# Zero matmuls in planned TensorE gaps, a new division of phi, and new due times, in a two-layer linear-attention and gated-MLP kernel

## The chip, the cores and the metric

The kernel runs on one core of one Trainium2 chip. The metric is device time in microseconds (us), median over runs. Every comparison is between runs of the same job on the same chip, unless it says otherwise.

Engines: PE is TensorE, ACT is ScalarE, DVE is VectorE, POOL is GpSimd, SP is SyncE, which here only issues DMAs. "Clock" is the TensorE clock that the chip granted, as a share of full speed.

## The reference

Two layers, each a linear attention A and a gated MLP B with residuals, on x of 2048 tokens by 512. Cut to what matters:

```python
qkv = x @ wqkv                                   # 32 heads of 16
pq, pk = q @ w_phi, k @ w_phi                    # per head
phi = concat([softmax(p), softmax(-p)])          # of pq and of pk
kv, z = phi_k^T v, sum over tokens of phi_k      # the "sum over tokens"
o = (phi_q kv) / (phi_q z + 1e-6);  A = o @ wo
B = (relu(x @ W_gate) * (x @ W_up)) @ W_down
x = x + A(layernorm(x)); x = x + B(layernorm(x))  # twice
```

The sum over tokens (named `kvz`) accumulates over all 16 tiles of 128 tokens before any query can be answered. Everything until then is the head of the kernel.

## The kernel before

The kernel records operations, each with a cost estimate and a due time. At build time a planner walks them in simulated time and picks, engine by engine, what goes next; the due times come from a search by annealing over that planner. On the chip only the resulting order counts, engine by engine.

```python
POOL_HEAD = 30.2
PHI = dict(POOL=[("POOL", 16)] * 4, DVE=[("DVE", 64)], BOTH=[("DVE", 32), ("POOL", 16), ("POOL", 16)])
PHI0 = ["POOL"] * 15 + ["BOTH"]     # who computes phi, for the 16 tiles of layer one
DUE = ( ... )                       # one due time per operation
# ...
    c_z = op("DVE", dve(512, 4), -9, lambda: nc.vector.memset(p_h.tiles[0][:, 0:512], 0.0), name="zero", port=True)
# ...
    wps = Buf(p_q)
    op("PE", mm(8, 512), 0, lambda: [nc.tensor.matmul(
        wps.t[:], lhsT=p_h.tiles[0][:, 0:P], rhs=p_h.tiles[0][:, 0:512],
        start=True, stop=True) for _ in range(8)], [c_z], [wps], name="warm")
# ... for each tile of 128 tokens: key product, exp on ACT (ek), sum (sk), 1/sum, then phi:
            for e, n in PHI[phi_eng]:
                q, cost = (nc.vector, dve(n * DH)) if e == "DVE" else (nc.gpsimd, (POOL_HEAD * n, POOL_HEAD * n + 10))
                parts.append(op(e, cost, due, lambda q=q, lo=lo, n=n: phi(q, lo, n), [a], [] if lo else [ph],
                                [ek, sk] + ([ph] if lo else []), name="phi", port=True))
                lo += n
# ... at the end:
    order = arrange(ops)
    with tc.manual_schedule():
        for o in order:
            o.emit()
```

The eight `warm` matmuls of zeros keep PE active while the first data are loaded (1.19 to 4.79 us in the trace, 0.43 us apart). In layer one GpSimd does phi in four instructions of 16 heads per tile, and in the last tile VectorE takes half. (The code counts 64 heads to a tile: each of the 32 heads of the reference stands there twice, once for each of its two softmaxes.)

The softmax here doesn't subtract the row's maximum and nothing guards it: scores larger than these inputs give would overflow.

## Time and profile before

| | before |
|---|---|
| three runs | 396.55 us median (396.2 to 397.12) |
| the profiled run | 398.66 us, span 396.9 us, mean clock 0.991 |
| matmuls of 512 columns, start to start | 0.43 us at clock 0.50, 0.216 us at 1.00 |

The page of the kernel before: the span, the busy line of PE (busy us, share, instructions), and from the 40 slices the PE line and the clock line, where 9 is 90% or more.

```profile
span 396.9 us, 7609 instructions
...
PE 381.3 (96%) x2780; PEld 232.0 (58%) x2827; DVE 269.9 (68%) x663; ACT 257.1 (65%) x683; POOL 40.7 (10%) x72
...
PE   8799899999999999999999999999899999999996
...
PEclk9699999999999999999999999999999999999999
...
PE 81%; ACT 8%; DMA 5%; DVE 4%; issue 1%; DVEq 0%; ACTq 0%
```

PE is busy nearly always and makes up 81% of the chain of waits (the last line). The second slice of the clock line has a 6: there the clock was not full. A caution for the PE count: this trace has 2780 matmul records and 2827 weight loads, so 47 matmul records are missing, and small gaps without a named wait are not to be believed.

The table of stretches for the dip (stretch, length, busy us of PE, PEld, DVE, ACT and POOL with the instruction count of each, then the clock, the DMA share and GB/s; PEld is the loading of weights into TensorE):

```profile
8.64:12.05 3.41, 1.62 (x12) 0.55 (x9) 3.41 (x11) 2.54 (x9) 0.00 (x0) 1.00 0.57 108
12.05:15.47 3.42, 2.23 (x13) 1.42 (x13) 3.28 (x6) 2.06 (x9) 1.32 (x3) 0.50 0.19 41
15.47:18.88 3.41, 3.41 (x11) 1.18 (x9) 2.64 (x5) 1.55 (x3) 1.03 (x2) 0.50 0.73 212
```

In the first stretch PE was busy for 1.62 of 3.41 us. In the following two it ran at half clock. The stretches follow the clock record of this trace, which changes at 5.21, 12.04 and 18.86 us. A stretch of 3.41 us is called a window here. The timeline of PE (start, length, line, what, and in brackets the idle time before it with what ended it) shows the gaps and the slow matmuls:

```profile
8.29 0.59 PE L663 MATMUL b<-Wk,xnTA 128*128 128x512 bf16 x2
9.17 0.38 PE L663 MATMUL b<-Wk,xnTA 128*128 128x512 bf16 x1 [0.28 <-ACT Wk L587]
9.73 0.38 PE L663 MATMUL b<-Wk,xnTA 128*128 128x512 bf16 x1 [0.18 <-DVE Wk L587]
11.43 0.72 PE L623 MATMUL b<-ident,xn 128*128 128x128 bf16 x8 [1.33 <-DVE xn L643]
13.34 1.49 PE L663 MATMUL b<-Wk,xnTA 128*128 128x512 bf16 x3 [1.19 <-ACT rsA L640]
...
17.18 1.86 PE L663 MATMUL b<-Wk,xnTA 128*128 128x512 bf16 x4
```

The group of four key products at 17.18 took 1.86 us; elsewhere such a group takes 1.03 us. The waits of PE over the whole run (what waited, for what, us in total, times, longest):

```profile
PE b L783 <- DMA oT<-o: 2.2, 3, 1.0
PE b L736 <- DMA xnTA<-xn: 1.5, 1, 1.5
PE b L623 <- DVE xn L643: 1.3, 1, 1.3
PE b L663 <- ACT rsA L640: 1.2, 1, 1.2
PE q L580 <- DVE hT L560: 1.2, 1, 1.2
PE b L783 <- ACT oT L587: 1.0, 2, 0.6
...
```

All lines of this list together make 9.5 us.

### The profile page before, as it was taken

The page shows a single profiled execution, that of the slowest core. Times are in us where ns is not written, and L with a number is a line of the kernel's source. Part 1 is how long each engine was busy: PE and PEld are TensorE (multiplying, and loading weights), DVE is VectorE, ACT ScalarE, POOL GpSimd, SP SyncE. Part 2 cuts the span into 40 slices and gives each one's busy share as a digit, 9 for nine tenths or more (in the row PEclk, how much of TensorE's full clock was granted, in tenths as well). Part 3 has the DMA queues.
Part 4 walks back from the last instruction along what each step waited for, and adds up shares of the span by engine and source line. Part 5 has one row for each costly group of instructions (what it writes and reads, how often), then busy time and mean ns, then how long its engine had stood idle before and what let it go on. Part 6 is the DMA issues. An engine that isn't in the chain of part 4 may idle for free.

```text
span 396.9 us, 7609 instructions
## 1 busy us (share of the span) xinstructions
PE 381.3 (96%) x2780; PEld 232.0 (58%) x2827; DVE 269.9 (68%) x663; ACT 257.1 (65%) x683; POOL 40.7 (10%) x72
## 2 busy tenths in 40 slices
PE   8799899999999999999999999999899999999996
PEld 4354555876655454646666655577675444547585
DVE  6898645889958797953575887778799881322232
ACT  5699999975656557654646769997565545164141
POOL 0286891000000000000000002000000000000000
PEclk9699999999999999999999999999999999999999
DMA  8339760122423311210102000013333512101110
GB/s 238 104 90 192 197 195 0 25 52 49 93 28 67 42 40 40 41 20 15 29 20 55 0 15 0 2 28 61 67 61 80 99 24 28 59 0 28 40 49 28
DMA packets 60870, 22.84 MB, mean 58 GB/s; under 512 B 52672, under 2 KB 59808, under 8 KB 60832
## 3 DMA queue, kind: packets, MB, share of 16 engines
q1 hardware_dynamic: 60416, 21.95, 25.2%
q8 instruction: 22, 0.36, 0.4%
q10 hardware_dynamic: 416, 0.39, 0.3%
q14 instruction: 16, 0.13, 0.1%
HBM read 7.91 MB, written 2.10 MB: 25 GB/s over the span
## 4 chain that ended last, share of the span: by engine, by line
PE 81%; ACT 8%; DMA 5%; DVE 4%; issue 1%; DVEq 0%; ACTq 0%
PE b L847 32%; PE b L881 18%; PE b L663 6%; PE b L669 6%; PE b L783 5%; PE b L736 4%; PE q L699 3%; DMA oT<-o 3%; PE b L823 3%; PE q L754 2%; ACT Eq L740 2%; ACT N L761 2%; DMA xnTA<-xn 1%; ACT DS L761 1%; ACT ek L666 1%
## 5 line engine op out<-in xcount | busy, mean ns | idle before, releaser
L847 PE MATMUL b<-xnTB,wgu 128*128 128x128 bf16 (+2 forms) x1194 | 151.6, 279 | 0.4
L847 PEld LDWEIGHTS <-wgu 128*128 128x128 bf16 x1200 | 98.0, 98 | 45.9 <-issue 0.3
L881 PE MATMUL b<-wd,hT 128*128 128x512 bf16 (+2 forms) x344 | 83.4, 372 | 1.0
L851 ACT ACTIVATE gu<-b 128x512 bf16<-128x512 f32 x83 | 49.9, 605 | 39.3 <-PE b L847 39.2
L854 ACT CAST gu<-b 128x512 bf16<-128x512 f32 (+1 forms) x83 | 48.8, 590 | 36.3 <-PE b L847 35.8
L857 DVE TENSOR_TENSOR hT<-gu 128x512 bf16<-128x512 bf16 (+1 forms) x83 | 34.0, 411 | 43.0 <-ACT gu L854 42.7
L683 POOL TENSOR_TENSOR phiK<-ek,sk 128x256 bf16<-128x256 bf16 x66 | 40.0, 639 | 203.8 <-ACT sk L679 198.3
L881 PEld LDWEIGHTS <-hT 128*128 128x128 bf16 (+1 forms) x363 | 34.3, 98 | 31.2 <-DVE hT L857 0.4
L674 DVE TENSOR_REDUCE sk<-ek 128x64 f32<-128x1024 bf16 x32 | 38.7, 1213 | 19.9 <-ACT ek L666 19.7
L761 ACT CAST N<-q 128x384 bf16<-128x384 f32 (+1 forms) x96 | 44.4, 531 | 4.9 <-PE q L754 3.8
L888 DVE SCALAR_TENSOR_TENSOR X<-b,rsB,X 128x512 bf16<-128x512 f32 (+1 forms) x33 | 23.5, 726 | 26.2 <-PE b L881 26.1
L666 ACT ACTIVATE ek<-b 128x512 bf16<-128x512 f32 x64 | 36.0, 604 | 8.2 <-PE b L663 8.0
L740 ACT ACTIVATE Eq<-b 128x512 bf16<-128x512 f32 x64 | 37.8, 657 | 1.6 <-PE b L736 1.2
L663 PE MATMUL b<-Wk,xnTA 128*128 128x512 bf16 x124 | 33.7, 393 | 1.8 <-ACT rsA L640 1.2
L783 PE MATMUL b<-wo,oT 128*128 128x512 bf16 x119 | 31.6, 379 | 3.6 <-DMA oT<-o 2.2
L669 PE MATMUL b<-wv,xnTA 128*128 128x512 bf16 x125 | 32.8, 387 | 0.2
L736 PE MATMUL b<-xnTA,Wq 128*128 128x512 bf16 x122 | 30.6, 379 | 1.8 <-DMA xnTA<-xn 1.5
L754 PE MATMUL q<-R,Eq 128*128 128x144 bf16 x256 | 26.3, 226 | 0.2
L787 DVE TENSOR_TENSOR X<-X,b 128x512 bf16<-128x512 bf16 x32 | 21.7, 678 | 6.7 <-PE b L783 5.8
L754 PEld LDWEIGHTS <-Eq 128*128 128x128 bf16 x256 | 19.8, 98 | 9.2 <-issue 0.4
L761 ACT COPY DS<-q 128x48 f32<-128x48 f32 (+1 forms) x96 | 20.2, 276 | 6.1 <-PE q L754 3.7
L632 DVE BATCH_NORM_STATS2 bstA<-X 128x6 f32<-128x512 bf16 x32 | 21.4, 684 | 2.6 <-DMA X<-in_A_x_dram 2.2
(66 smaller groups left out, 367.6 us busy)
## 6 DMA issues: line engine op xcount, KB each, us to landing
out_dram<-X SPq DMA_DIRECT2D x15, 128.0 KB, 1.7
X<-in_A_x_dram SPq DMA_DIRECT2D x6, 256.0 KB, 3.2
wgu<-in_B_W_gate_dram SPq DMA_DIRECT2D x4, 344.0 KB, 3.6
wgu<-in_B_W_up_dram SPq DMA_DIRECT2D x4, 344.0 KB, 3.7
wd<-in_B_W_down_dram SPq DMA_DIRECT2D x5, 256.0 KB, 4.0
wv<-in_A_wqkv_dram SPq DMA_DIRECT2D x2, 256.0 KB, 4.6
wo<-in_A_wo_dram SPq DMA_DIRECT2D x4, 128.0 KB, 3.3
oT<-o SPq DMA_TRANSPOSE x28, 2.4
```

The source lines that it names most:

```text
L663: k = op("PE", mm(4, 512), due, lambda: [nc.tensor.matmul(kp.t[:], lhsT=xnTA[c][:, b, cols], rhs=Wk2[:, b, :], start=(b == 0), stop=(b == ...
L669: v = op("PE", mm(4, 512), due_v, lambda: [nc.tensor.matmul(vp.t[:], lhsT=xnTA[c][:, b, cols], rhs=wv[:, b, :], start=(b == 0), stop=(b == ...
L683: e.tensor_tensor(out=ph.t[:].rearrange("p s (h f) -> p (s h) f", f=DH)[:, lo:lo + n], in0=ek.t[:].rearrange("p s (h f) -> p (s h) f", f=D ...
L736: q = op("PE", mm(4, 512), due(c, b), lambda b=b, qp=qp: [nc.tensor.matmul(qp.t[:], lhsT=Wq2[:, m, b * P:(b + 1) * P], rhs=xnTA[c][:, m, : ...
L740: done.append(op("ACT", act(512), due(c, b), lambda b=b, s=s, qp=qp: nc.scalar.activation(out=Eq[c][:, b, s, :], in_=qp.t[:], func=AF.Exp, ...
L754: pe.append(op("PE", mm(len(groups), GE), due, lambda ps=ps, groups=groups: [nc.tensor.matmul(ps.t[:, n * GE:(n + 1) * GE], lhsT=Eq[c][:, ...
L761: nc.scalar.copy(out=q[:, k, 0:3] if k < 2 else q[:, :, 3], in_=ps.t[:, 0:n * GE].rearrange("p (n c j) -> p n c j", n=n, j=HB)[:, :, lo:hi])
L783: a = op("PE", mm(4, 512), due + 3, lambda: [nc.tensor.matmul(yp.t[:], lhsT=oT.t[:, b, :], rhs=wo[:, b, :], start=(b == 0), stop=(b == NB ...
L847: nc.tensor.matmul(ps.t[:, q * W:(q + 1) * W], lhsT=wgu[:, s, b, g * P:(g + 1) * P], rhs=xT.t[:, b, 0:W], start=(b == 0), stop=(b == NB - 1))
L851: nc.scalar.activation(out=gu.t[:, 0, 0:cols], in_=gp.t[:, 0:cols], func=AF.Relu)
L854: nc.scalar.copy(out=gu.t[:, 1, 0:cols], in_=up.t[:, 0:cols])
L881: nc.tensor.matmul(yp.t[:, 0:c1 - c0], lhsT=h.t[:m, f * W + i * P:f * W + (i + 1) * P], rhs=wd[:m, f, c0:c1], start=(f == 0), stop=(f == N ...
```

## The change

Three things at once. (1) After planning, wherever PE has a planned gap before the first sum over tokens, the kernel emits as many zero matmuls of 512 columns as fit ("fillers"); the intent is to leave PE no idle time there. (2) Phi on GpSimd goes in two halves of 32 heads, and every third tile of layer one goes to VectorE whole. (3) New due times, annealed for this.

```diff
-POOL_HEAD = 30.2
+FILL = 216
-PHI = dict(POOL=[("POOL", 16)] * 4, ...)
-PHI0 = ["POOL"] * 15 + ["BOTH"]
+PHI = dict(POOL=[("POOL", 32)] * 2, ...)
+PHI0 = ["POOL", "POOL", "DVE"] * 5 + ["BOTH"]
 DUE = ( ... )                                   # all values replaced
-    eps = new("eps", [1], F32)
+    eps, zero = new("eps", [1], F32), new("zero", [512])
-    c_z = ... memset(p_h.tiles[0][:, 0:512], 0.0)
+    c_z = ... memset(zero[:], 0.0)
+    def idle(n):
+        for _ in range(n):
+            nc.tensor.matmul(wps.t[:], lhsT=zero[:, 0:P], rhs=zero[:], start=True, stop=True)
-    op("PE", mm(8, 512), 0, lambda: [... for _ in range(8)], [c_z], [wps], name="warm")
+    op("PE", mm(8, 512), 0, lambda: idle(8), [c_z], [wps], name="warm")
-... else (nc.gpsimd, (POOL_HEAD * n, POOL_HEAD * n + 10))
+... else (nc.gpsimd, (28.6 * n + 120, 28.6 * n + 150))
     with tc.manual_schedule():
+        free, filling = None, True
         for o in order:
+            if o.eng == "PE":
+                filling = filling and o.name != "kvz"
+                if filling and free is not None:
+                    idle(max(0, int((o.start - free - 150) / FILL)))
+                free = o.start + o.spent
             o.emit()
```

In the built program this gives nine fillers: six before the first key product and three before the second. The other instructions of PE are the same in number, in another order.

## The prediction

> **What bounds the kernel now.** TensorE. The page has PE busy 381.3 of 396.9 us, and the chain of waits puts 81% of the span on PE. But part of it is at half speed. The table of stretches shows granted clock 0.50 from 12.05 to 18.88 us, and 1.00 from there on. Matmuls of 512 columns are 0.43 us apart there, 0.216 us elsewhere. The timeline shows why: PE was busy only 1.62 us from 8.64 to 12.05 us (1.3 us of idle for the VectorE scaling of x, then 1.2 us for the ScalarE chain). [...] A window that was 61% busy (39.4 to 42.8 us) kept the full clock, one that was 47% busy lost it.

> From 20 to 80 us ScalarE is nearly full as well (about 57 of 60 us); PE has gaps there of 1.5 us (39.1 to 40.65, for the transposing DMA of the normalized x) and 1.4 us in all from 60 to 80. Later: 1.8 us of DMA waits before output projections (279 and 313 us), and 2.5 us of drain at the end.

> **What the change does.**
> 1. Nine zero matmuls: six after the fold before the first key product, three before the second and third. That is 9 x 0.216 = 1.9 us, where PE idled about 3 us. The stretch 8.64 to 12.05 should rise from 1.6 to roughly 3 us busy, so the clock stays full. PE's work between 13.34 and 18.88 us took 5.5 us; at full clock it takes about half: 2.7 us gained. The second pair of normalizations also moves ahead of one statistics instruction (0.66 us). Gain in the head: 2.7 to 3.8 us.
> 2. GpSimd phi: 2 instructions of 32 heads in place of 4 of 16 (0.59 us apart, 2.35 us per tile); five of the tiles go to VectorE (1.22 us each, as in layer two). GpSimd falls from about 40 to about 25 us busy, VectorE gains 6 us, which it has after 40 us. PE waited for no phi, so this alone is worth about nothing.
> 3. New due times reorder everything. PE's real work is unchanged. I expect the 1.5 us gap at 39 us to go, and some of the rest to move, because ScalarE has the same work and was full there. Net 0 to 2 us.

> On the critical path: item 1 nearly whole, since PE is saturated after it, if ScalarE gets its work earlier too (busy 6.4 us from 10 to 20).

> **Prediction: 392.4 us, range 389.2 to 395.4 (8 in 10).** Faster by over 2%: 0.09; within 2%: 0.89; slower by over 2%: 0.02.

> **What shows it right.** Granted clock 1.00 in all slices after the first warm-up; matmuls at 0.216 us from 12 to 19 us; no 1.5 us gap at 39 us; GpSimd busy about 25 us; PE's busy time falls by 1 to 3 us (fillers add 1.9).

> **What makes it wrong.** Fillers that come too early and leave an empty window anyway; ScalarE or VectorE taking the lead from 20 to 60 us, so that the head's gain returns as PE gaps between 40 and 80 us; new DMA waits in the second half from the new order; or an order that closes most later gaps, giving over 8 us.

That the clock stays full rests on the two stretches measured, 61% busy (full clock kept) and 47% busy (clock lost).

## The result and the profile after

| | before | after |
|---|---|---|
| six runs each, same job | 396.38 us median (395.12 to 397.12) | 393.11 us median (392.93 to 393.26) |
| ratio | | 0.9921, 95% interval 0.9904 to 0.9937 |
| profiled run: span, clock | 396.9 us, 0.991 | 391.3 us, 1.0 |

A ratio is the mean time of one kernel's fast runs over that of the other's fast runs of the same rounds, so it is not quite the ratio of the medians quoted beside it.

Two things stand out at once. The runs of the kernel after lie within 0.33 us, those of the kernel before within 2.0 us. And the two profiled runs differ by 5.6 us in span, while the medians differ by only 3.3 us: the profiled run of before, at 398.66 us, was slower than every other run of that kernel (the next is 398.47 us).

The page after, the same lines:

```profile
span 391.3 us, 7634 instructions
...
PE 383.4 (98%) x2836; PEld 232.7 (59%) x2836; DVE 272.9 (70%) x668; ACT 256.1 (65%) x683; POOL 27.6 (7%) x32
...
PE   8999998999999999999999999999999999999996
...
PEclk9999999999999999999999999999999999999999
...
PE 85%; ACT 8%; DVE 3%; DMA 2%; issue 1%; DVEq 0%
```

The clock line has no dip. The same stretches after:

```profile
8.64:12.05 3.41, 3.27 (x23) 1.51 (x21) 3.41 (x11) 2.80 (x9) 0.00 (x0) 1.00 0.48 110
12.05:15.47 3.42, 3.39 (x22) 1.59 (x21) 3.42 (x8) 3.26 (x10) 0.00 (x0) 1.00 0.89 85
15.47:18.88 3.41, 3.41 (x25) 1.77 (x23) 3.41 (x7) 3.38 (x12) 2.07 (x2) 1.00 0.56 178
```

PE is busy 3.27 us of the first stretch in place of 1.62, and the clock stays at 1.00. The timeline of PE in the head, with the fillers on line L560:

```profile
8.61 1.46 PE L560 MATMUL q<-zero 128*128 128x512 bf16 x6
9.90 1.03 PE L643 MATMUL b<-Wk,xnTA 128*128 128x512 bf16 x4
11.07 0.72 PE L603 MATMUL b<-ident,xn 128*128 128x128 bf16 x8
11.62 0.81 PE L560 MATMUL q<-zero 128*128 128x512 bf16 x3
12.47 1.90 PE L643 MATMUL b<-Wk,xnTA 128*128 128x512 bf16 x8
...
16.93 1.90 PE L643 MATMUL b<-Wk,xnTA 128*128 128x512 bf16 x8
```

Now eight key products take 1.90 us, as long as four took before. The waits of PE after:

```profile
PE q L560 <- DVE zero L537: 1.3, 1, 1.3
PE q L734 <- ACT N L741: 1.1, 2, 0.7
PE b L763 <- ACT oT L567: 0.9, 2, 0.6
PE b L643 <- DMA xnTA<-xn: 0.4, 1, 0.4
PE b L763 <- DMA oT<-o: 0.3, 1, 0.3
...
```

The whole list makes 4.5 us, in place of 9.5. The sum for the two profiled runs closes: 5.0 us less waiting; 2.8 us less for the work that ran at half clock (PE was busy 2.23 + 3.41 = 5.6 us there, half of which is 2.8); the nine fillers add 9 x 0.216 = 1.9 us. That makes 5.9 us; the spans differ by 5.6 us. But this sum holds for a slow run of before, and it lumps the three parts of the change together. The experiments take them apart.

**Theories.** A, the clock: the gain is the half-clock stretch avoided by the fillers. B, the order: the gain is shorter waits from the new due times, and the fillers are incidental. C, phi: GpSimd was a hidden limit.

### The profile page after: what moved, and what is told of

The parts are those of the page before. It is cut to its first block, busy times and chain, and to the rows that moved or that the text cites. A ratio compares the mean times of both kernels' runs of the same rounds, so it can differ in the third digit from the quotient of the medians.

```text
span 391.3 us, 7634 instructions
## 1 busy us (share of the span) xinstructions
PE 383.4 (98%) x2836; PEld 232.7 (59%) x2836; DVE 272.9 (70%) x668; ACT 256.1 (65%) x683; POOL 27.6 (7%) x32
## 4 chain that ended last, share of the span: by engine, by line
PE 85%; ACT 8%; DVE 3%; DMA 2%; issue 1%; DVEq 0%
PE b L827 35%; PE b L861 19%; PE b L763 6%; PE b L643 6%; PE b L649 5%; PE b L716 4%; PE q L679 3%; PE b L803 3%; PE q L734 3%; ACT Eq L720 2%; ACT N L741 2%; ACT ek L646 2%; DMA xnTA<-xn 1%; PE q L560 1%; DMA oT<-o 1%
## 5 line engine op out<-in xcount | busy, mean ns | idle before, releaser
L827 PE MATMUL b<-xnTB,wgu 128*128 128x128 bf16 (+2 forms) x1200 | 149.2, 279 | 0.1
L831 ACT ACTIVATE gu<-b 128x512 bf16<-128x512 f32 (+1 forms) x83 | 49.2, 605 | 32.4 <-PE b L827 31.7
L663 POOL TENSOR_TENSOR phiK<-ek,sk 128x512 bf16<-128x512 bf16 (+1 forms) x26 | 26.9, 1056 | 213.0 <-ACT sk L659 203.4
L720 ACT ACTIVATE Eq<-b 128x512 bf16<-128x512 f32 x64 | 39.2, 667 | 3.7 <-PE b L716 3.5
L763 PE MATMUL b<-wo,oT 128*128 128x512 bf16 x128 | 32.6, 379 | 1.1 <-ACT oT L567 0.9
L643 PE MATMUL b<-Wk,xnTA 128*128 128x512 bf16 x128 | 32.1, 379 | 0.4 <-DMA xnTA<-xn 0.4
L716 PE MATMUL b<-xnTA,Wq 128*128 128x512 bf16 x128 | 31.5, 379 | 0.1
L741 ACT COPY DS<-q 128x48 f32<-128x48 f32 (+1 forms) x96 | 22.3, 284 | 10.2 <-PE q L734 8.6
L663 DVE TENSOR_TENSOR phiK<-ek,sk 128x1024 bf16<-128x1024 bf16 (+1 forms) x22 | 25.3, 1162 | 3.3 <-ACT sk L659 1.7
```

Of the source, the lines that this page charges most:

```text
L643: k = op("PE", mm(4, 512), due, lambda: [nc.tensor.matmul(kp.t[:], lhsT=xnTA[c][:, b, cols], rhs=Wk2[:, b, :], start=(b == 0), stop=(b == ...
L663: e.tensor_tensor(out=ph.t[:].rearrange("p s (h f) -> p (s h) f", f=DH)[:, lo:lo + n], in0=ek.t[:].rearrange("p s (h f) -> p (s h) f", f=D ...
L716: q = op("PE", mm(4, 512), due(c, b), lambda b=b, qp=qp: [nc.tensor.matmul(qp.t[:], lhsT=Wq2[:, m, b * P:(b + 1) * P], rhs=xnTA[c][:, m, : ...
L720: done.append(op("ACT", act(512), due(c, b), lambda b=b, s=s, qp=qp: nc.scalar.activation(out=Eq[c][:, b, s, :], in_=qp.t[:], func=AF.Exp, ...
L741: nc.scalar.copy(out=q[:, k, 0:3] if k < 2 else q[:, :, 3], in_=ps.t[:, 0:n * GE].rearrange("p (n c j) -> p n c j", n=n, j=HB)[:, :, lo:hi])
L763: a = op("PE", mm(4, 512), due + 3, lambda: [nc.tensor.matmul(yp.t[:], lhsT=oT.t[:, b, :], rhs=wo[:, b, :], start=(b == 0), stop=(b == NB ...
```

## The experiments

Twelve runs in three jobs of four. All results were correct against the reference. Each job ran the kernel before 11 times beside them: 396.28, 396.18 and 397.45 us median.

| run | what it is | median us | ratio to before |
|---|---|---|---|
| no_fill | after, without fillers | 394.64 | 0.9964 |
| fill_only | before, with fillers | 394.21 | 0.9954 |
| phi_only | before, with new phi | 398.16 | 1.0053 |
| before_again | before | 396.53 | 1.001 |
| after_again | after | 393.2 | 0.9911 |
| quarters | after, phi on GpSimd in 16 heads | 393.15 | 0.9917 |
| all_pool | after, layer-one phi all on GpSimd | 393.86 | 0.9939 |
| phi_fill | before, with new phi and fillers | 395.75 | 0.9978 |
| after_third | after | 393.43 | 0.9926 |
| no_fill_again | after, without fillers | 395.48 | 0.9971 |
| six_only | after, first six fillers only | 393.82 | 0.9931 |
| double_fill | after, 18 fillers | 394.26 | 0.9935 |

### How large is the clock term? The kernel before, run again

No edit.

> The kernel before, unchanged, for the clock and time of each of its runs. If the half-clock stretch causes its spread (395.1 to 398.7 us so far): the mean granted clock differs between runs and the longer runs have the lower clock, by about 0.5 us of time for each 0.0025 of clock (1 us at half clock). If not: clock equal, times unordered.

Its six runs took 395.67 to 396.85 us, all with clock 0.995 or 0.996, so within this run there was nothing to compare. The runs of before that stood beside the experiments give the answer, together with these six. There are 39, and they fall into three groups:

| mean clock | runs | mean time, us | range |
|---|---|---|---|
| 0.999 to 1.000 | 10 | 395.18 | 394.47 to 396.03 |
| 0.995 to 0.996 | 25 | 396.74 | 395.67 to 398.10 |
| 0.991 | 4 | 398.07 | 397.88 to 398.47 |

One window of 3.41 us at half clock lowers the mean by 3.41 x 0.5 / 395 = 0.0043, so the groups are none, one and two windows lost. The trace of this run has one, from 12.87 to 16.28 us. These are its stretches before and in that window:

```profile
9.45:12.87 3.42, 1.30 (x11) 0.54 (x10) 3.42 (x11) 3.00 (x11) 0.00 (x0) 1.00 0.48 109
12.87:16.28 3.41, 3.41 (x15) 1.78 (x16) 3.00 (x7) 2.09 (x5) 2.28 (x4) 0.50 0.23 46
```

A lost window costs 1.3 to 1.6 us by these groups. They mix three chips; within the three jobs the gap between none and one is 1.3, 1.3 and 2.5 us. The rate in the expectation (0.5 us for each 0.0025 of clock, 0.9 us for 0.0043) was too low, by its own arithmetic: 1 us at half clock takes only 0.5 / 395 = 0.0013 from the mean. On average the runs of before lose 396.47 - 395.18 = 1.3 us this way, not the 2.8 us of the run that was profiled first. Two traces suggest that where the windows lie decides which group a run falls into (the other runs have no trace): the clock records of the traces put the end of the first half-clock period at 5.21 us in the first trace of before and at 6.04 us in this one, with later changes at whole multiples of 3.41 us from there (12.04 and 18.86 us; 12.87 and 16.28 us). In this second trace the same two gaps lie across the window edges differently, and only one window is lost. The window after the first loss tells the two apart: in the first trace PE was busy for 2.22 us of it (12.04 to 15.45 us, 65%) and the clock stayed at half for one more, in this one for all of it (12.87 to 16.28 us) and the full clock came back.

### The fillers alone

```diff
 # the kernel before, its due times and its phi untouched
+FILL = 216
+    eps, zero = ...          # and idle(n), as in the change
         for o in order:
+            if o.eng == "PE": ...   # the same loop as in the change
             o.emit()
```

> The kernel before, order and phi untouched, with zero matmuls in its own planned gaps (5, 3 and 3 of them). If the clock is the gain: clock 1.00 after the warm-up, time 393 to 394 us, spread under 0.5 us. If the new order is the gain: about 396.4 us or slower by the fillers' 2.4 us.

It has eleven fillers, for its own gaps. 394.21 us, ratio 0.9954 (0.9932 to 0.9976), clock 0.999 or 1.0 in all six runs; five of them lie between 393.96 and 394.35 us, one took 395.47 us. So fillers in the old order win about 1.8 us, over half of the change. Theory A stands as a part. The time lies just beyond the slow edge of what A expected. It is also 0.9 us less (by the means, 394.4 and 395.3 us) than the four runs of before in the same job that lost no window; none of those was profiled, so the cause of that part is open. The trace of before_again, which lost one window, can be laid beside that of fill_only, one PE record to one. At 11.3 us fill_only is 0.6 us later, at 16.4 us it is 1.1 us ahead, and at the end 1.5 us; the last step, 0.4 us, stands at 276 us, where before_again waits 0.31 us for a transposing DMA. So not all of the gain arises in the head.

### The new order without fillers

```diff
-                    idle(max(0, int((o.start - free - 150) / FILL)))
+                    idle(0)
```

> The changed kernel without its nine zero matmuls after the first eight; order otherwise untouched. If the fillers keep the clock and the clock is the gain: PE is about 1.8 us busy of 3.4 between 8.6 and 12 us, clock 0.50 from about 12 us for one or two windows of 3.4 us, time 395 to 396.5 us with a spread of over 1 us between runs. If the new order is the gain: clock stays mostly full or does not matter, time 392.5 to 393.5 us.

> The changed kernel without its nine fillers, beside it on one chip. It was 394.6 us in a run apart, although the clock fell in only one of six runs. If fillers act through the clock alone: its runs with clock 1.00 equal the changed kernel beside it within 0.4 us, and only runs with 0.996 are 1 us or more slower. If the fillers act otherwise too (a shift that changes which DMA lands late): runs with clock 1.00 are again 1 us or more slower, and the waits for transposing DMAs are the longer ones in its trace.

First 394.64 us, ratio 0.9964 (0.9942 to 0.9987); clock 0.999 or 1.0 in five runs of six, so on that chip the new order alone mostly kept the clock. The time lies between what A and B expected. Then, beside the changed kernel (after_third), 395.48 against 393.43 us; four of its six runs had 0.996. The two of its runs that kept the clock, 394.91 and 395.33 us, were still 1.5 and 1.9 us slower than that median. So the fillers act otherwise than through the clock as well, and the pure form of theory A falls.

Where is the time? The order of both kernels is the same, so their PE records can be laid side by side one for one. Without fillers the first sum over tokens starts at 19.63 us, with them at 19.64 us: the fillers cost nothing, they lie in real gaps. From the second matmul of the first key product until 80 us the two stay within 0.2 us of each other, except around 35 to 42 us, where the version without fillers is up to 0.7 us ahead. Then one wait makes a step. PE with fillers (after_third):

```profile
80.68 1.04 PE L763 MATMUL b<-wo,oT 128*128 128x512 bf16 x4 [0.20 <-DMA oT<-o]
```

PE without (no_fill_again):

```profile
82.03 1.04 PE L763 MATMUL b<-wo,oT 128*128 128x512 bf16 x4 [1.37 <-DMA oT<-o]
```

This output projection waits for a transposing DMA. It was issued at 77.70 us with fillers and at 77.88 us without, so it landed later by more than it was issued later. Beside it, another transfer shows in the DMA records: a block of 16 KB on the queue of kind "instruction". From all nine traces of the changed order:

| trace | transposing DMA issued, us | 16 KB instruction block, us | issue to the projection's start, us |
|---|---|---|---|
| after | 77.64 | 77.87 to 79.10 | 3.07 |
| after_again | 77.45 | 77.69 to 78.62 | 3.00 |
| after_third | 77.70 | 77.96 to 79.07 | 2.98 |
| quarters | 77.31 | 77.67 to 78.63 | 3.23 |
| all_pool | 78.10 | 78.38 to 79.42 | 3.14 |
| double_fill | 78.62 | 78.72 to 79.65 | 2.75 |
| no_fill | 77.50 | 78.78 to 79.83 | 3.73 |
| no_fill_again | 77.88 | 79.05 to 80.36 | 4.16 |
| six_only | 77.41 | 78.32 to 79.88 | 4.11 |

Where all nine fillers stand, or more, the block starts within 0.4 us of the issue and the projection starts within 3.23 us. Where fillers are missing, the block starts 0.9 to 1.3 us after the issue, before the transposition has landed, and it takes 3.7 us or more. The traces of the kernels before and after have 22 such blocks each. The records do not name their engine, but the count points to one: in the trace of the kernel after, 5400 matmuls and weight loads start between the first block and the last, 257 to a block, while VectorE and ScalarE have 668 and 683 instructions in all. So the author takes them to carry PE's program; no record shows it. Nine fillers are 18 instructions of PE (a weight load and a matmul each). If the blocks follow the count, leaving them out moves the later blocks; in the table the block then starts 0.9 to 1.3 us after the issue in place of 0.1 to 0.4.

Is this more than a coincidence of nine? All fourteen traces have 1414 transposing DMAs. Of the 1063 without a block from 1.5 us before their issue to 3 us after it, half landed within 2.43 us and 95% within 3.3 us. Of the 109 where a block started 0.9 to 2.0 us after the issue, none landed in under 3.34 us, and half took over 4.04 us. Waiting behind another transfer does not explain it: among those with no other DMA issued from 3 us before to 2 us after, 114 without a block took 2.39 to 3.10 us, and nine with one took 3.34 to 4.38 us. So a block in that place goes with some 1.6 us more, everywhere in the kernel. That is a strong association, not an experiment. Fillers of one column in the same places, which would keep the number of instructions and take away the activity, were not run. So it stays unproved that the block causes the 1.2 us step (82.03 - 80.68 = 1.35 us apart at the projection, 0.19 us apart at the group before it). If it does, this part of the fillers' worth is luck: where a block starts beside a transfer differs with 18 instructions more or less. A second, smaller step of the same kind, 0.25 us, stands at 276 us, at a wait for another transposing DMA.

### Which fillers, and how many

```diff
-                    idle(max(0, int((o.start - free - 150) / FILL)))
+                    k = max(0, int((o.start - free - 150) / FILL))          # six_only
+                    idle(k if k > 3 else 0)                                 # six_only
+                    idle(2 * max(0, int((o.start - free - 150) / FILL)))    # double_fill, in its place
```

> The changed kernel with only the six fillers before the first key product, not the three before the second. If the six are what counts (they fill the longer gap): within 0.4 us of the changed kernel, clock 1.00. If all are needed: between it and the version without fillers, 393.6 to 394.6 us.

> The changed kernel with twice the fillers (12 and 6), 9 x 0.216 = 1.9 us more of TensorE in the head. If the head of TensorE is on the critical path: 1.0 to 1.9 us slower than the changed kernel, 394.1 to 395.1 us, and the sums over tokens start that much later. If the head has slack (ScalarE is the limit from 15 to 60 us): under 0.6 us slower.

> The changed kernel once more, as the yardstick on the chip of the three runs beside it: 392.5 to 393.6 us, clock 1.00 in all runs.

The yardstick after_third took 393.43 us, as expected, though two of its six runs lie at 394.05 and 394.42 us.

six_only: 393.82 us, clock 0.999 or 1.0 in all runs, 0.4 us slower than the yardstick by the medians and 0.3 us by the means, which is within the noise. Six fillers are enough for the clock. In its trace the wait at 81.5 us is 1.33 us, as without any fillers:

```profile
81.52 1.04 PE L763 MATMUL b<-wo,oT 128*128 128x512 bf16 x4 [1.33 <-DMA oT<-o]
```

But that trace is of its slowest run, 394.54 us, 1.2 us above the profiled run of the yardstick. Its other five took 393.6 to 394.21 us, so most of them can hardly have had the whole step: it need not be the same from run to run.

double_fill: 394.26 us, 0.8 us slower by the medians and 0.4 us by the means (394.09 and 393.67 us), for 1.9 us of additional matmuls. Its first sum over tokens starts at 20.92 us, 1.3 us later than in the yardstick, and its first attention product at 61.47 us, 0.9 us later than the yardstick's 60.53 us. The head is thus on the critical path in part: of 1.9 us of matmuls 0.9 us are left where the attention begins. "1.0 us or more" was missed; whether "under 0.6 us" was met depends on medians or means, and the intervals (0.9902 to 0.9968, and 0.9889 to 0.9962 for the yardstick) do not decide it.

### Phi

phi_only takes the new division of phi into the kernel before, with its due times (entries of dropped pieces left out); phi_fill adds the fillers.

```diff
 # the kernel before
-PHI = dict(POOL=[("POOL", 16)] * 4, ...);  PHI0 = ["POOL"] * 15 + ["BOTH"]
+PHI = dict(POOL=[("POOL", 32)] * 2, ...);  PHI0 = ["POOL", "POOL", "DVE"] * 5 + ["BOTH"]
     # due times: n-th operation takes its own old entry, entries of pieces that no longer exist are skipped
```

> The kernel before with the new division of phi alone, old due times, no fillers. Both theories: within 1 us of 396.4 us, half clock from 12 to 19 us as before. If GpSimd was the hidden limit: 394 us or less.

> The kernel before with the new phi and with zero matmuls in its own planned gaps, but the old due times: everything of the change but the annealing. If the annealing gives the rest of the gain: clearly slower than the changed kernel, 395 to 397.5 us (the new phi with old due times left a 2.2 us DMA wait at 40 us, and the fillers stop before it). If phi and fillers suffice: 393 to 394 us.

phi_only: 398.16 us, ratio 1.0053 (1.0014 to 1.0092), and a spread from 395.74 to 400.98 us. Both theories had expected a time within 1 us of 396.4 us, and missed. The new phi in the old order costs time. Part of it is lost clock: its two runs that kept the clock (395.74 and 396.62 us) are 0.9 us slower than the four such runs of before. The trace (the run of 400.98 us, clock 0.987) shows how:

```profile
42.67 1.89 PE L666 MATMUL b<-Wk,xnTA 128*128 128x512 bf16 x4 [2.25 <-DMA xnTA<-xn]
```

PE waits 2.25 us for a transposing DMA of the normalized x, and the four key products after it take 1.89 us: the clock was lost a second time. In the first trace of before the like wait was 1.50 us. The DMA was issued at 36.36 us in place of 35.35, after VectorE had one phi more (1.22 us at 31.55 us), and it took 6.27 us to land in place of 5.25. A weight load is just ahead of it in the queue in both traces, and an instruction block beside it (39.33 to 41.57 us here, 38.56 to 39.65 there). So VectorE's added work can explain at most the 1.0 us of later issue; the other 1.0 us passes in the transfer. The stretch of that window:

```profile
39.16:42.58 3.42, 1.26 (x12) 0.73 (x10) 2.95 (x8) 2.47 (x11) 0.36 (x1) 1.00 1.16 142
```

PE was busy 1.26 of 3.42 us, and the clock record is at one half from 42.58 to 45.99 us. Theory C falls.

phi_fill: 395.75 us, ratio 0.9978 (0.9953 to 1.0003), clock 1.0 in all runs. With phi and fillers in place, the old due times leave it about 2.5 us behind the changed kernel of the same job (after_again, 393.2 us). It waits for transposing DMAs of the normalized x for 1.9 us in all; the changed kernel (first trace) waits 0.4:

```profile
PE b L670 <- DMA xnTA<-xn: 1.0, 2, 0.6
PE b L745 <- DMA xnTA<-xn: 0.9, 1, 0.9
```

So the new order is worth about 2.5 us once phi has been divided anew. That is theory B's share. Two things besides the due times differ: phi_fill has eleven fillers, not nine, and so its instruction blocks fall elsewhere too.

The next two keep the order of the changed kernel exactly and change only what is emitted.

```diff
-    lambda q=q, lo=lo, n=n: phi(q, lo, n)
+    lambda q=q, lo=lo, n=n: [phi(q, i, 16) for i in range(lo, lo + n, 16)] if q is nc.gpsimd else phi(q, lo, n)   # quarters
+    lambda q=q, lo=lo, n=n: [phi(nc.gpsimd, i, 32) for i in (0, 32)] if self.l == 0 and n == 64 else phi(q, lo, n)  # all_pool
```

> The changed kernel, unchanged, on the chip of the three runs beside it. If the fillers make the time independent of where the clock's windows fall: six runs within 0.5 us of each other at 392.9 to 393.4 us, clock 1.00 in all, while the kernel before spreads over 2 us in two groups (clock 1.000 near 395.3 us, clock 0.996 near 396.6 us).

> The changed kernel, same order, but each GpSimd phi of 32 heads cut into two of 16 (four per tile, about 2.4 us in place of 2.07 us). If no wait of TensorE ends on phi: 393.1 us as the changed kernel, within 0.4 us, and GpSimd about 4 us busier. If the halves pay by bringing phi sooner: 0.5 us or more slower.

> The changed kernel, same order, but the five VectorE tiles of the first layer's phi given to GpSimd in halves. VectorE loses 6 us of work, GpSimd gains 10 us. If the VectorE share is needed by the new order: PE waits for phi at sums over tokens, 394 us or more. If it is not: 392.5 to 393.3 us.

after_again: 393.2 us, ratio 0.9911, clock 0.999 or 1.0 in all runs. The spread on this chip was 1.4 us (392.3 to 393.66), wider than the 0.5 us expected, and not in the clock.

quarters: 393.15 us, ratio 0.9917. Cutting the halves in two costs nothing; the halves themselves win nothing. (GpSimd was 2.7 us busier, 30.3 in place of 27.6 us, where about 4 was expected.)

all_pool: 393.86 us, ratio 0.9939 against 0.9911 of the unchanged one: some 0.7 to 1.1 us slower, just short of the 394 us expected of a needed share. The intervals overlap, the single runs hardly do (393.48 to 395.17 us, and 392.3 to 393.66). Its waits of PE have a line that the changed kernel lacks:

```profile
PE q L680 <- POOL phiK L663: 0.8, 2, 0.5
```

The first of these two waits, 0.49 us, is at 45.2 us. So the share of VectorE is of use in the new order; in the old one (phi_only) the new division only cost time.

## Why the prediction was right

**The time.** 392.4 us was forecast, 393.11 us measured, inside the range of 389.2 to 395.4 us; "within 2%" was right.

**The clock (item 1): mechanism right, size off.** The fillers do keep the clock: it was 0.999 or 1.0 in all 18 runs of the changed kernel, and in all 54 runs with fillers of any number; without them 29 of 39 runs of before lost it, and 9 of 18 of the other kernels. The term that was mis-sized is "2.7 us gained", and with it "Gain in the head: 2.7 to 3.8 us". It was read from one trace, which happened to have lost two windows. Over 39 runs the kernel before loses 1.3 us on average to lost windows. The forecast took that trace as typical, but with 10, 25 and 4 of 39 runs that lost none, one and two windows, a single trace is a sample.

**The order (item 3): right, at the upper end.** "Net 0 to 2 us" was forecast. What the change wins (ratios 0.9911 to 0.9926, so about 3.2 us) less the 1.3 us of the clock leaves about 1.9 us. The too large first term and a low middle of this one cancelled; that the sum came out so near is luck. The 1.5 us gap at 39 us did go: a wait of 0.4 us is left of it. But the 1.9 us is a remainder, and not all of it is the order's. Without fillers, among runs that kept the clock, the new order was 0.8 us faster than before in one job (five runs and four) and 0.4 us slower in the other (two and three). With fillers on both sides, the ratios of the changed kernel and of fill_only differ by 1.1 to 1.7 us, across jobs, and about two thirds of that is VectorE's share of phi (all_pool). Part of the gain depends on the fillers in a way that was not forecast: without them the same order loses 1.2 us at one transposing DMA, in step with an instruction block on the DMA queues.

**Phi (item 2): wrong.** "PE waited for no phi, so this alone is worth about nothing." Alone it cost 1.9 us by the medians (ratio 1.0053). The step that failed is from "PE waited for no phi" to "about nothing". No wait of PE named phi in the kernel before, but with the new division PE waited 2.25 us for a transposition issued 1.0 us later, and in that run a clock window was lost as well. How much of this is VectorE's added work, and how much the DMA's own 1.0 us, is not shown. In the new order the division is worth 0.7 to 1.1 us, all of it from VectorE's share.

**Busy times.** GpSimd was to fall to about 25 us; it fell from 40.7 to 27.6 us. PE's busy time was to fall by 1 to 3 us; it rose from 381.3 to 383.4 us. The 381.3 was too low because 47 matmul records are missing in that trace; the second trace of before, complete, has 383.1 us. Against that the rise is 0.3 us: the nine fillers add 1.9 us, and one window at full clock in place of half saves about 1.7 us (3.41 x 0.5, an estimate). The forecast fall needed two lost windows in the kernel before.

**ScalarE.** Its work does come earlier: 9.3 us busy between 10 and 20 us, where it had 6.4 us. This was the condition for item 1 to be kept, and it held.

## What to carry to other kernels

## What the traces show of the clock and of the instruction blocks

- The clock fell after windows that were far from idle: PE was busy 1.26, 1.30, 1.52 and 1.63 us of 3.42 us (37 to 48%) in the four windows, the drains at the ends aside, after which the clock went from full to half (39.16 to 42.58 us in phi_only, 9.45 to 12.87 us in before_again, 8.44 to 11.86 us in phi_only, 8.62 to 12.04 us in the first trace of before). It was kept after windows with 1.95 us (57%, 36.76 to 40.17 us in before_again) and 2.05 us (60%, 39.34 to 42.75 us in the first trace of before). No share between was read in these traces.
- A window at half clock with PE busy for 2.22 us (65%, 12.04 to 15.45 us in the first trace of before) did not bring the full clock back; those with 3.41 us did (15.45 to 18.86 us there, 12.87 to 16.28 us in before_again). In phi_only PE was busy for 2.72 us (80%) from 12.05 to 15.47 us at clock 0.50, and the clock was still 0.53 in the 3.41 us after that. Counted in busy time, to regain the clock took more in these traces than to keep it.
- A window lost after the start costs 0.3 to 0.4% (1.3 to 1.6 us of 395). That decides a comparison of this size: 10, 25 and 4 of 39 runs of one kernel lost none, one and two windows.
- The clock record of the first trace of before changes at 5.21, 12.04 and 18.86 us, that of the kernel after first at 6.84 us. The half-clock stretches lasted 6.83 us in the first trace of before, 3.41 us in before_again (12.87 to 16.28 us) and 3.41 us in phi_only (42.58 to 45.99 us).
- Of 109 transposing DMAs with a 16 KB block 0.9 to 2.0 us after their issue, half took over 4.04 us to land, in place of 2.43 us without a block. Whether the wait reaches TensorE depends on the place: the one at 77.88 us in no_fill_again came with a wait of 1.37 us. The cause is not proved here.
